# A convolution block and a gated FFN on one core: h of the first and last block in two halves of rows, eleven loads on another queue, another order of first loads

## The chip, the core and the metric

The kernel runs on one core of a Trainium2 chip. The metric is device time in microseconds of one execution, the median over several. The core has a matrix engine (PE; PEld is its weight load), a vector engine (DVE), a scalar engine (ACT), GpSimd (POOL) and SyncE (SP). SP and POOL issue DMAs here, each engine runs its own instructions in the order in which they were built, and an instruction that waits holds up all that stand behind it on its engine.

## What is computed

```python
def _A_ref(q, k, v, shift_k, ssm_k, ssm_D):
    k_shift = sum(k_pad[:, t:t + S, :] * shift_k[:, ks - 1 - t] for t in range(ks))   # 4 taps
    kv = k_shift * v
    y = irfft(rfft(kv, 2S) * rfft(ssm_k, 2S))[:S]     # long causal convolution over the sequence
    y = y + kv * ssm_D
    return q * y

x = A_q                                                 # 2048 x 640
h = x + _A_ref(_layernorm(x), A_k, A_v, A_shift_k, A_ssm_k, A_ssm_D)
h2 = h + (silu(LN(h) @ w_gate) * (LN(h) @ w_up)) @ w_down    # 640 -> 1728 -> 640
```

All arrays are bfloat16. x, k, v are 2048 x 640, ssm_k is 640 x 2048. (B_x is not used.)

## The kernel before

The sequence is cut into four blocks of 512 tokens. A block is held as 128 partitions with 4 rows of 640 each; `ROWS = (1, 3, 0, 2)` is the order in which rows are handled. The convolution is done block by block in a transformed domain. For block j: the kernel piece g (of ssm_k) is turned (`g_turned`, line 396) and transformed (`spectrum`, line 436: G0 to G2; `window_of` for the last); k is loaded transposed into `kT`, the four taps and the product with v are formed (`kv_of`, line 480) and transformed (X0 to X3); `mac` (line 520) multiplies and adds the spectra of all pairs of blocks on DVE, and some of its additions are accumulating DMAs from POOL (`added`, line 234, issued at line 235); `inverse` (line 600) transforms back on PE (i0 to i3, L645), ACT scales each row (z, L652), DVE forms h = (x - mean) * z (L654) with its sum, ACT sums the squares (L568), `ln2` (line 590) makes the layernorm's scale with three small DVE operations and one power on POOL (L572); `turn_h` (line 661) normalizes each row (DVE L668 or ACT L666) and turns it into `hT`, by PE and an eviction for blocks 0 and 3, by DMA transposes for blocks 1 and 2 (`HTURN`). `ln1` (line 574) gets the layernorm of x on ACT and POOL.

`ffn(j)` then multiplies hT by gate and up weights (`proj`, L702: 5 matmuls of 512 columns, one for each 128 of the 640 channels) into PSUM pairs, two chunks of 128 features at once; ACT takes Silu (L714); the product with up goes either through an ACT copy (L717) and DVE (L719) or straight from PSUM on DVE (L718); the down projection (L749) takes 28 matmuls of 320 columns for each row. For blocks 0 to 2 h is stored first and the FFN's output is added to it in DRAM by accumulating DMAs from POOL (L756); the last block's rows are added on DVE (L766, L768) and stored from SP.

A name in `SUM` with 'four' (here i1 to i3, G0 to G2, X1 to X3) uses a form with half as many matmuls and more DVE additions (lines 613 to 634); a name in `DIRECT` (i0, X0) uses matmuls alone.

All operations are declared to a planner (`Plan`) that only replays them: `ORDER` is a list of operation numbers, written out, and each engine gets its instructions in that order. A negative number takes the operation's second form (an eviction on DVE instead of ACT, an addition by DMA instead of on DVE). Loads and stores (`load`, line 237) have one form here and are all issued by SP. Large tiles live in an arena of `UNITS` slots; PSUM has 4 slots of two banks.

Of the kernel before, what the change touches and what calls it, by code (L numbers as in the profile page):

```python
# [16 lines left out]
D = 640  # L17
# [18 lines left out]
DIRECT = ('i0','X0')  # L36
SUM = {'G0':'four','X1':'four','G1':'four','G2':'four','X2':'four','X3':'four','i1':'four','i2':'four','i3':'four'}
# [4 lines left out]
UNITS = 20  # L42
SLOTS = {"row": 4, "z": 2, "sg": 3, "ps": 4, "sm": 10}
ORDER = (
# [40 lines left out]
WHOLE = ((0, 1),)  # L85
ROWS = (1, 3, 0, 2)

# [96 lines left out]
def kernel(ctx: ExitStack, tc: tile.TileContext, A_q, A_k, A_v, A_shift_k, A_ssm_k, A_ssm_D, B_x,  # L184
# [52 lines left out]
    def load(nbytes, fn, w, r=()):  # L237
        return plan.add("sp", nbytes / 370.0, fn, r, w)
# [36 lines left out]
    def load_g(j):  # L275
        b = new("ld")
        load(MB, lambda: nc.sync.dma_start(
            out=ap(b).rearrange("p (c t) -> p c t", c=KT),
            in_=A_ssm_k[0:D, j * BLK:(j + 1) * BLK].rearrange("(c p) t -> p c t", p=P)), [b])
        return b  # L280

    def load_t(src, j):
        b = new("ld")
        load(MB, lambda: nc.sync.dma_start(out=rd(b), in_=block(src, j)), [b])
        return b

    def load_x(j):
        b = new("x")
        load(MB, lambda: nc.sync.dma_start(out=ap(b), in_=block(xq, j)), [b])
        return b  # L290
# [178 lines left out]
    def load_k(j):  # L469
# [5 lines left out]
        for lo in (0, 2):  # L475
            load(MB // 2, lambda lo=lo: nc.sync.dma_start(out=rd(k)[:, lo:lo + 2], in_=block(kk, j)[:, lo:lo + 2, :]), [(k, lo // 2)])
# [418 lines left out]
```

## Time and profile before

| what | value |
|---|---|
| median of 3 runs | 267.63 us (265.11 to 268.7) |
| the profiled execution | 265.97 us |
| its span, first to last instruction | 264.3 us |
| mean granted PE clock | 0.987 |
| busy: DVE, ACT | 204.4 us, 172.5 us |
| DMA | 34.22 MB, mean 130 GB/s |

A line of the profile names source line, engine, operation, tiles and count; the numbers behind are total busy time in us and mean duration in ns, then the idle time ahead of those instructions and what ended it. "Critical" pieces (the chain of waits) give start, length and what ran. PE busy times overlap, since matmuls are pipelined; the pace is read from runs of back-to-back matmuls.

### The profile page before, as it was taken

How to read it: one execution, taken by the hardware profiler on the slowest of the kernel's cores; microseconds unless marked ns; L12 is line 12 of the kernel's file. 1: busy time of each engine (PE TensorE's matmuls, PEld its weight loads, DVE VectorE, ACT ScalarE, POOL GpSimd, SP SyncE). 2: the span in 40 equal slices, each digit the busy share in tenths (PEclk: the TensorE clock that was granted, in tenths of full speed). 3: DMA queues.
4: the chain of work that ended last, by engine and by line, in shares of the span. 5: the costliest groups of instructions: out<-in, count | busy, mean ns of one | idle time of the engine just before them, and what ended most of it. 6: DMA issues, size and time to landing. Idle time of an engine off the chain costs nothing.

```text
span 264.3 us, 4769 instructions
## 1 busy us (share of the span) xinstructions
PE 240.2 (91%) x1914; PEld 138.8 (53%) x1929; DVE 204.4 (77%) x271; ACT 172.5 (65%) x294; POOL 48.8 (18%) x52
## 2 busy tenths in 40 slices
PE   2588989699999999999957999999999999999993
PEld 2455655444455676444423777544456764444771
DVE  3579969899999999998998999999999430222113
ACT  1798999897797994247777974775595834533100
POOL 2000130102122131330061021213228203000000
PEclk9999999799999999999997999999999999999999
DMA  6946899995584527789237906697491225000002
GB/s 220 355 133 104 227 350 218 289 249 99 102 278 146 99 102 148 134 186 145 37 99 127 227 0 139 152 195 127 89 149 14 38 25 72 5 0 0 0 29 74
DMA packets 37731, 34.22 MB, mean 130 GB/s; under 512 B 22406, under 2 KB 32716, under 8 KB 37708
## 3 DMA queue, kind: packets, MB, share of 16 engines
q1 hardware_dynamic: 32716, 24.08, 34.2%
q0 software_dynamic: 4992, 9.83, 23.2%
q8 instruction: 15, 0.25, 0.4%
q14 instruction: 8, 0.07, 0.1%
HBM read 16.21 MB, written 4.59 MB: 79 GB/s over the span
## 4 chain that ended last, share of the span: by engine, by line
PE 41%; DVE 32%; DMA 11%; ACT 7%; issue 6%; SPq 2%; DVEq 0%; ACTq 0%
PE ps L702 21%; DVE arena L524 17%; PE ps L749 13%; PE ps L317 4%; DMA arena<-in_A_v_dram 3%; DMA arena<-arena 3%; DMA arena<-in_A_q_dram 3%; DVE arena L654 2%; ACT arena L400 2%; DMA arena<-in_A_ssm_k_dram 2%; DVE arena L367 2%; PE ps L645 2%; DVE arena L371 2%; PE ps L392 1%; DVE tT L719 1%
## 5 line engine op out<-in xcount | busy, mean ns | idle before, releaser
L702 PE MATMUL ps<-arena,wgu 128*128 128x512 bf16 x506 | 114.6, 379 | 1.2 <-DMA arena<-row 0.4
L524 DVE TENSOR_TENSOR arena<-arena 128x2560 bf16<-128x2560 bf16 (+1 forms) x68 | 91.4, 1369 | 1.5 <-DMA arena<-arena 0.8
L702 PEld LDWEIGHTS <-wgu 128*128 128x128 bf16 x520 | 50.6, 98 | 59.8 <-issue 0.9
L749 PE MATMUL ps<-wd,tT 128*128 128x320 bf16 x448 | 64.0, 299 | 0.9 <-DVE row L768 0.9
L749 PEld LDWEIGHTS <-tT 128*128 128x128 bf16 x448 | 43.6, 98 | 18.5 <-issue 1.1
L714 ACT ACTIVATE sg<-ps 128x1024 bf16<-128x1024 f32 (+1 forms) x28 | 26.8, 961 | 30.0 <-PE ps L702 24.9
L317 PE MATMUL ps<-arena,WF 128*128 128x320 bf16 x160 | 28.8, 302 | 6.8 <-DMA arena<-arena 2.7
L717 ACT CAST sg<-ps 128x1024 bf16<-128x1024 f32 (+1 forms) x23 | 21.9, 952 | 12.4 <-DVE tT L719 5.6
L719 DVE TENSOR_TENSOR tT<-sg,sg 128x1024 bf16<-128x1024 bf16 (+1 forms) x23 | 15.0, 652 | 17.1 <-ACT sg L717 17.1
L235 POOL DMA_DIRECT2D arena<-arena x12 | 14.8, 1307 | 68.3 <-DVE arena L524 27.8
L317 PEld LDWEIGHTS <-WF 128*128 128x128 bf16 x160 | 15.4, 99 | 17.1 <-issue 7.6
L568 ACT ACTIVATE junk<-arena 128x640 bf16<-128x640 bf16 x32 | 23.7, 742 | 0.9 <-DVE arena L654 0.4
L307 ACT CAST arena<-ps 128x320 bf16<-128x320 f32 (+1 forms) x44 | 22.8, 578 | 0.4 <-PE ps L317 0.4
L307 ACT ACTIVATE arena<-ps 128x640 bf16<-128x640 f32 (+1 forms) x29 | 18.6, 667 | 2.3 <-PE ps L317 1.9
L645 PE MATMUL ps<-arena,WI 128*128 128x320 bf16 x96 | 17.1, 320 | 2.8 <-DVE arena L623 2.7
L572 POOL TENSOR_TENSOR sm<-sm,neghalf 128x4 f32<-128x4 f32 x8 | 11.3, 1415 | 37.4 <-DVE sm L595 37.0
L652 ACT ACTIVATE z<-ps,sm 128x640 f32<-128x640 f32 x16 | 12.6, 805 | 4.7 <-POOL sm L572 2.0
L654 DVE SCALAR_TENSOR_TENSOR arena<-arena,sm,z 128x640 bf16<-128x640 bf16 x16 | 13.7, 880 | 1.6 <-ACT z L652 1.5
L583 POOL TENSOR_TENSOR sm<-sm 128x4 f32<-128x4 f32 x4 | 3.9, 966 | 56.9 <-ACT junk L578 56.9
L645 PEld LDWEIGHTS <-WI 128*128 128x128 bf16 x96 | 9.5, 102 | 8.8 <-DVE arena L623 4.0
L756 POOL DMA_DIRECT2D out_dram<-row x12 | 12.2, 1251 | 8.1 <-ACT row L754 8.1
L578 ACT ACTIVATE junk<-arena 128x640 bf16<-128x640 bf16 x16 | 11.9, 742 | 1.7 <-DMA arena<-in_A_q_dram 1.6
(77 smaller groups left out, 204.8 us busy)
## 6 DMA issues: line engine op xcount, KB each, us to landing
arena<-arena POOLq DMA_DIRECT2D x12, 640.0 KB, 6.2
arena<-in_A_q_dram SPq DMA_DIRECT2D x4, 640.0 KB, 5.7
arena<-in_A_v_dram SPq DMA_DIRECT2D x4, 640.0 KB, 7.9
arena<-in_A_ssm_k_dram SPq DMA_DIRECT2D x4, 640.0 KB, 7.0
wd<-in_B_w_down_dram SPq DMA_DIRECT2D x1, 2080.0 KB, 9.5
out_dram<-arena SPq DMA_DIRECT2D x3, 640.0 KB, 5.2
out_dram<-row POOLq DMA_DIRECT2D x12, 160.0 KB, 4.5
wgu<-in_B_w_up_dram SPq DMA_DIRECT2D x1, 800.0 KB
```

What stands on the lines that cost most here:

```text
L235: plan.add("dve", ns, fn, reads, [write], ("add", 2 * P * R * D, lambda: nc.gpsimd.dma_start(out=to(), in_=what(), accum_op=ALU.add, max_d ...
L307: (lambda: nc.scalar.activation(dst(), src(), ACT.Copy, scale=2.0)) if twice else (lambda: nc.scalar.copy(dst(), src())),
L317: nc.tensor.matmul(ap(ps)[:, h, 0:NH], w, ap(src)[:, r, h * NH:(h + 1) * NH], start=(first and i == 0), stop=(last and i == len(rs) - 1), ...
L524: return lambda: f(*(x() for x in args))
L568: act(725, lambda r=r: nc.scalar.activation(ap(junk), ap(x)[:, r, :], ACT.Square, scale=D ** -0.5, accum_out=sm(s, MSQ, (r,))), [(x, r)], ...
L645: nc.tensor.matmul(ap(ps)[:, w, 0:NH], m, src[:, w * NH:(w + 1) * NH], start=(i == 0), stop=(i == len(terms) - 1))
L654: dve(740, lambda r=r, z=z: v.scalar_tensor_tensor(ap(x)[:, r, :], ap(x)[:, r, :], sm(n1, MEAN, (r,)), ap(z), op0=ALU.subtract, op1=ALU.mu ...
L702: nc.tensor.matmul(ap(ps)[:, i, :], w(k), ap(hT)[:, k, :], start=(k == 0), stop=(k == KT - 1))
L714: act(905 if two_ else 490, lambda: nc.scalar.activation(of(sg), of(*gate), ACT.Silu), [(gate[0], gate[1] + i) for i in range(m)], [sg])
L717: op = plan.add("act", 905 if two_ else 490, lambda: nc.scalar.copy(of(co), of(*up)), psu + [sg], [co] + tt, ("dve", 1135 if two_ else 600 ...
L719: op.rest = dve(602 if two_ else 336, lambda: nc.vector.tensor_mul(to(), of(sg), of(co)), [sg, co], tt)
L749: nc.tensor.matmul(ap(ps)[:, hf, 0:NH], ap(tT)[:, c, at:at + P], ap(wd)[:, c, hf * NH:(hf + 1) * NH], start=(c == 0), stop=(c == NCH - 1))
```

## The change

1. For blocks 0 and 3 (`LEAD = {0: 4, 3: 2}`) `inverse` makes the statistics of h in two halves of two rows each, with a `sm` tile, three DVE operations and one power of their own, and `turn_h` uses them so. The first 4 (block 0) or 2 (block 3) groups of the gate and up projections are done on 256 tokens at a time: matmuls of 256 columns, two groups of features sharing a PSUM tile.
2. Every load has a second form issued by GpSimd (`"pq"`). ORDER takes it for eleven: x of blocks 1 to 3, v of block 1, g of block 2, one weight piece of 800 KB, both loads of `w_down`, the h store of block 1, and two output stores of the last block.
3. ORDER is a new list throughout. The first loads on SP are x, ssm_D, taps, g, WF (the transform's basis), k in two pieces, g of block 1, v, WI; before they were k, taps, k, x, v, g, g of block 1, ssm_D, WF, WI. The warm-up matmuls stand first on PE; before they stood between i0 and the FFN. In the new list five PSUM copies more are on ACT and fewer on DVE, and 13 additions instead of 12 are DMAs.
4. i1 is no longer 'four': 32 instead of 16 matmuls, without six DVE additions. The arena has 21 slots instead of 20.

In the whole program there are 120 matmuls of 512 columns less and 240 of 256 more, and 16 of 320 more.

```diff
-DIRECT = ('i0','X0')
-SUM = {'G0':'four','X1':'four','G1':'four','G2':'four','X2':'four','X3':'four','i1':'four','i2':'four','i3':'four'}
+DIRECT = ('X0', 'i0')
+SUM = {'G0': 'four', 'X1': 'four', 'G1': 'four', 'G2': 'four', 'X2': 'four', 'X3': 'four', 'i2': 'four', 'i3': 'four'}
...
-UNITS = 20
+LEAD = {0: 4, 3: 2}
+UNITS = 21
...
+HALVES = (ROWS[:2], ROWS[2:])
...
     def load(nbytes, fn, w, r=()):
-        return plan.add("sp", nbytes / 370.0, fn, r, w)
+        return plan.add("sp", nbytes, lambda: fn(nc.sync), r, w, ("pq", nbytes, lambda: fn(nc.gpsimd)))
...
-        s = new("sm")
-        for r, ps in out.items():
-            z = new("z")
...
-        square_sums(x, s, ROWS)
-        ln2(s, ROWS)
-        return s
+        stats = []
+        for rs in HALVES if LEAD.get(j) else (ROWS,):
+            s = new("sm")
+            for r in rs:
+                ps, z = out[r], new("z")
...
+            square_sums(x, s, rs)
+            ln2(s, rs)
+            stats += [(r, s) for r in rs]
+        return stats
...
+        lead = LEAD.get(j, 0)
...
+        def proj(ps, i, w, src, rs=ROWS):
+            lo, n = ROWS.index(rs[0]) * P, len(rs) * P
+
             def mm():
                 for k in range(KT):
-                    nc.tensor.matmul(ap(ps)[:, i, :], w(k), ap(hT)[:, k, :], start=(k == 0), stop=(k == KT - 1))
-            pe(1079, mm, src + [hT], [(ps, i)])
+                    nc.tensor.matmul(split(ap(ps), n)[:, i, :], w(k), ap(hT)[:, k, lo:lo + n], start=(k == 0), stop=(k == KT - 1))
+            pe(1079 if n == BLK else 546, mm, src + [(hT, r) for r in rs], [(ps, i)])
...
+        def chunks(gis, rs):
             g, u = new("ps"), new("ps")
...
+            for b, gi in enumerate(gis):
+                for a, ps in enumerate((g, u)):
+                    for i in range(2):
+                        f0 = (2 * gi + i) * P
+                        proj(ps, 2 * b + i, lambda k, a=a, f0=f0: ap(wgu)[:, k, a, f0:f0 + P], [(wgu, (group(f0), a))], rs)
+            gate_up(2 * gis[0], 2 * len(gis), (g, 0), (u, 0), rs)
...
+        for gi in range(0, lead, 2):
+            chunks((gi, gi + 1), HALVES[0])
+        if j == 0:
+            for gi in range(0, lead, 2):
+                chunks((gi, gi + 1), HALVES[1])
+        for gi in range(lead, NGRP - 1):
+            chunks((gi,), ROWS)
+        odd_chunks()
+        if j:
+            for gi in range(0, lead, 2):
+                chunks((gi, gi + 1), HALVES[1])
```

ORDER's new list is left out here, and so are the many calls of `load` that only hand on the queue.

More of the change, by code (lines that the diff above doesn't have):

```diff
@@ L283, in load_t @@
         b = new("ld")
-        load(MB, lambda: nc.sync.dma_start(out=rd(b), in_=block(src, j)), [b])
+        load(MB, lambda q: q.dma_start(out=rd(b), in_=block(src, j)), [b])
         return b
@@ L288, in load_x @@
         b = new("x")
-        load(MB, lambda: nc.sync.dma_start(out=ap(b), in_=block(xq, j)), [b])
+        load(MB, lambda q: q.dma_start(out=ap(b), in_=block(xq, j)), [b])
         return b
@@ L475, in load_k @@
         for lo in (0, 2):
-            load(MB // 2, lambda lo=lo: nc.sync.dma_start(out=rd(k)[:, lo:lo + 2], in_=block(kk, j)[:, lo:lo + 2, :]), [(k, lo // 2)])
+            load(MB // 2, lambda q, lo=lo: q.dma_start(out=rd(k)[:, lo:lo + 2], in_=block(kk, j)[:, lo:lo + 2, :]), [(k, lo // 2)])
         for r in range(R):
@@ L662, in turn_h @@
+        return stats
+    def turn_h(x, stats, j):
         hT = new("hT")
-        for r in ROWS:
+        for r, s in stats:
             hn = new("row")
             at = ROWS.index(r)
-            plan.add("act", 815, lambda r=r, hn=hn: nc.scalar.activation(ap(hn), ap(x)[:, r, :], ACT.Identity, bias=sm(s, OFF, (r,)), scale=sm(s, RSTD, (r,))),
+            plan.add("act", 815, lambda r=r, hn=hn, s=s: nc.scalar.activation(ap(hn), ap(x)[:, r, :], ACT.Identity, bias=sm(s, OFF, (r,)), scale=sm(s, RSTD, (r,))),
@@ L693, in ffn, with split @@
         if not end:
-            load(MB, lambda: nc.sync.dma_start(out=block(oo, j), in_=ap(h)), [there], [h])
+            load(MB, lambda q: q.dma_start(out=block(oo, j), in_=ap(h)), [there], [h])
         def done(cs, rs):
             return (tT, frozenset((c, r) for c in cs for r in rs))
-        def proj(ps, i, w, src):
+        lead = LEAD.get(j, 0)
+        def split(t, n):
+            return t.rearrange("p a (b n) -> p (a b) n", n=n)
+        def proj(ps, i, w, src, rs=ROWS):
+            lo, n = ROWS.index(rs[0]) * P, len(rs) * P
@@ L706, in gate_up @@
             sg, co = new("sg"), new("sg")
+            lo, n = ROWS.index(rs[0]) * P, len(rs) * P
             def of(b, at=0):
-                return ap(b)[:, at:at + m, :]
+                return split(ap(b), n)[:, at:at + m, :]
             def to():
-                return ap(tT)[:, c:c + m, :]
-            two_ = m == 2
-            act(905 if two_ else 490, lambda: nc.scalar.activation(of(sg), of(*gate), ACT.Silu), [(gate[0], gate[1] + i) for i in range(m)], [sg])
+                return ap(tT)[:, c:c + m, lo:lo + n]
@@ L715, in gate_up @@
+            wide_ = m * n > BLK
+            act(905 if wide_ else 490, lambda: nc.scalar.activation(of(sg), of(*gate), ACT.Silu), [(gate[0], gate[1] + i) for i in range(m)], [sg])
             psu = [(up[0], up[1] + i) for i in range(m)]
-            tt = [done(range(c, c + m), ROWS)]
-            op = plan.add("act", 905 if two_ else 490, lambda: nc.scalar.copy(of(co), of(*up)), psu + [sg], [co] + tt,
-                          ("dve", 1135 if two_ else 600, lambda: nc.vector.tensor_mul(to(), of(sg), of(*up))))
@@ L730, in ffn @@
-        for a in range(2):
-            proj(ps, a, lambda k, a=a: ap(wgu)[:, k, a, f0:f0 + P], [(wgu, (group(f0), a))])
-        gate_up(NC_FULL - 1, 1, (ps, 0), (ps, 1))
-        last_ps, sg, up = new("ps"), new("sg"), new("sg")
-        proj(last_ps, 0, lambda k: ap(wodd)[:, k], [wodd])
-        act(490, lambda: nc.scalar.activation(ap(sg)[0:64, 0, :], ap(last_ps)[0:64, 0, :], ACT.Silu), [(last_ps, 0)], [sg])
-        act(490, lambda: nc.scalar.copy(ap(up)[0:64, 0, :], ap(last_ps)[64:P, 0, :]), [(last_ps, 0)], [up])
@@ L737, in ffn @@
-        dve(336, lambda: nc.vector.tensor_mul(ap(tT)[0:64, NC_FULL, :], ap(sg)[0:64, 0, :], ap(up)[0:64, 0, :]), [sg, up], [done([NC_FULL], ROWS)])
+            tt = [done(range(c, c + m), rs)]
+            op = plan.add("act", 905 if wide_ else 490, lambda: nc.scalar.copy(of(co), of(*up)), psu + [sg], [co] + tt,
+                          ("dve", 1135 if wide_ else 600, lambda: nc.vector.tensor_mul(to(), of(sg), of(*up))))
+            op.rest = dve(602 if wide_ else 336, lambda: nc.vector.tensor_mul(to(), of(sg), of(co)), [sg, co], tt)
@@ new lines, in chunks, with odd_chunks @@
+        def chunks(gis, rs):
+            g, u = new("ps"), new("ps")
+            for b, gi in enumerate(gis):
[4 more added lines that the diff above has]
+            gate_up(2 * gis[0], 2 * len(gis), (g, 0), (u, 0), rs)
+        def odd_chunks():
+            ps = new("ps")
+            f0 = (NC_FULL - 1) * P
+            for a in range(2):
+                proj(ps, a, lambda k, a=a: ap(wgu)[:, k, a, f0:f0 + P], [(wgu, (group(f0), a))])
+            gate_up(NC_FULL - 1, 1, (ps, 0), (ps, 1))
+            po, sg, up = new("ps"), new("sg"), new("sg")
+            proj(po, 0, lambda k: ap(wodd)[:, k], [wodd])
+            act(490, lambda: nc.scalar.activation(ap(sg)[0:64, 0, :], ap(po)[0:64, 0, :], ACT.Silu), [(po, 0)], [sg])
+            act(490, lambda: nc.scalar.copy(ap(up)[0:64, 0, :], ap(po)[64:P, 0, :]), [(po, 0)], [up])
+            dve(336, lambda: nc.vector.tensor_mul(ap(tT)[0:64, NC_FULL, :], ap(sg)[0:64, 0, :], ap(up)[0:64, 0, :]), [sg, up], [done([NC_FULL], ROWS)])
@@ L769, in ffn @@
                 dve(740 if len(hs) == 2 else 407, out_of, [(ps, hf) for hf in hs] + [(h, r), (n1, cells(MEAN, (r,)))], [(o, hf) for hf in hs])
[L770 removed]
+                load(MB // 4 // (3 - len(hs)), lambda q, r=r, o=o, lo=lo, n=n: q.dma_start(out=block(oo, j)[:, r, lo:lo + n], in_=ap(o)[:, lo:lo + n]),
                      [], [(o, hf) for hf in hs])
@@ L794 @@
     dve(350, fold, [ident], [eye])
-    load(P * KT * 8, lambda: nc.sync.dma_start(out=ap(taprow), in_=A_shift_k.rearrange("(c p) t -> c (p t)", p=P)), [taprow])
+    load(P * KT * 8, lambda q: q.dma_start(out=ap(taprow), in_=A_shift_k.rearrange("(c p) t -> c (p t)", p=P)), [taprow])
     pt = new("ps")
@@ L812 @@
     x = load_x(0)
-    load(P * R * 4 * P * 2, lambda: nc.sync.dma_start(out=ap(WI), in_=wi_h.ap()), [WI])
+    load(P * R * 4 * P * 2, lambda q: q.dma_start(out=ap(WI), in_=wi_h.ap()), [WI])
     minus = new("minus")
```

37 lines of the change are left out of this document (13 added, 24 removed), and 82 rows, old and new, of the table ORDER.

## The prediction, made before the changed kernel was run

> **What bounds the kernel now.** I read the page's totals first, then the windows of 10 us, then the chain of waits, and last the timeline of the first 54 us.
>
> ```profile
> span 264.3 us, 4769 instructions
> ...
> PE 240.2 (91%) x1914; PEld 138.8 (53%) x1929; DVE 204.4 (77%) x271; ACT 172.5 (65%) x294; POOL 48.8 (18%) x52
> ```
>
> ```profile
> 10.00:20.00 10.00, 6.63 (x66) 4.18 (x67) 7.96 (x19) 9.84 (x22) 0.00 (x0) 1.00 0.65 215
> ...
> 30.00:40.00 10.00, 8.96 (x174) 6.32 (x167) 7.62 (x11) 9.83 (x17) 3.41 (x4) 1.00 1.16 331
> ...
> 130.00:140.00 10.00, 7.26 (x34) 3.15 (x32) 9.90 (x12) 8.44 (x12) 5.44 (x5) 0.92 0.21 66
> 140.00:150.00 10.00, 8.16 (x156) 5.35 (x155) 9.03 (x16) 8.58 (x15) 0.00 (x0) 0.91 0.96 182
> ...
> 190.00:200.00 10.00, 9.95 (x57) 5.47 (x57) 9.86 (x9) 9.10 (x17) 4.88 (x5) 1.00 0.63 100
> ...
> 220.00:230.00 10.00, 9.95 (x47) 4.58 (x47) 1.11 (x2) 4.67 (x6) 2.29 (x3) 1.00 0.40 51
> ```
>
> The columns are busy times of PE, PEld, DVE, ACT and POOL, then PE's clock, the DMA share and GB/s. There are three stages with three limits. Up to 50 us ACT is full (9.84 and 9.83 of 10). From there to 200 us DVE is full and PE nearly so. After 200 us DVE is almost empty and PE alone is full. The chain of waits gives PE's true pace, since each of its pieces is a back-to-back run:
>
> ```profile
> 64.42 10.76 PE ps L702 x49
> ...
> 77.77 1.11 PE ps L489 x112
> ...
> 131.51 4.75 DMA arena<-in_A_ssm_k_dram
> 136.33 2.52 ACT arena L400
> ...
> 200.78 0.72 PE ps L645 x4
> ...
> 205.58 6.52 PE ps L749 x48
> 212.10 0.56 PE ps L392 x10
> ...
> 260.83 0.55 DVE row L768
> ```
>
> So a matmul of 512 columns takes 10.76/49 = 0.2196 us, one of 320 takes 6.52/48 = 0.1358, a transpose 0.056, a tap 0.0099. The row at 200.78 is the first matmul of i3, the inverse transform of the last block; DVE work ends just ahead of it, and PE runs from there to the end. I therefore cut the span at two points: S, the first FFN matmul, and I, the first matmul of i3.
>
> ```profile
> 2.11 0.52 POOL L781 MEMSET tT<- 64x512 bf16 x1
> ...
> 8.83 0.74 ACT L578 ACTIVATE junk<-arena 128x640 bf16<-128x640 bf16 x1 [1.57 <-DMA arena<-in_A_q_dram]
> ...
> 28.72 0.52 SPq L284 DMA_DIRECT2D arena<-in_A_v_dram  x1
> ...
> 30.04 0.50 SPq L289 DMA_DIRECT2D arena<-in_A_q_dram  x1
> ...
> 31.91 0.81 POOL L583 TENSOR_TENSOR sm<-sm 128x4 f32<-128x4 f32 x1 [29.29 <-ACT junk L578]
> ...
> 40.04 0.88 DVE L654 SCALAR_TENSOR_TENSOR arena<-arena,sm,z 128x640 bf16<-128x640 bf16 x1
> ...
> 44.98 0.88 DVE L654 SCALAR_TENSOR_TENSOR arena<-arena,sm,z 128x640 bf16<-128x640 bf16 x1
> ...
> 53.52 3.40 PE L702 MATMUL ps<-arena,wgu 128*128 128x512 bf16 x14
> ```
>
> S is 53.5. Between S and I lie 147.3 us. In the built order that stretch holds 405 matmuls of 512, 358 of 320 (254 of the down projection, 72 forward, 32 inverse) and 280 taps: 88.9 + 48.6 + 2.8 = 140.3 us. PE loses 7.0 us there. After I lie 63.5 us with 135 of 512, 210 of 320 and 20 transposes: 29.6 + 28.5 + 1.1 = 59.3 us, and 4.2 of tail.
>
> **The last block (LEAD 3: 2).** In the changed order, after I stand 95 matmuls of 512, 80 of 256, 182 of 320 and 20 transposes. A matmul of 256 is not in the trace. Its floor is half of 512, 0.110. Its ceiling is that plus a weight load that is not hidden:
>
> ```profile
> L702 PEld LDWEIGHTS <-wgu 128*128 128x128 bf16 x520 | 50.6, 98 | 59.8 <-issue 0.9
> ...
> L626 DVE TENSOR_TENSOR arena<-arena 128x640 bf16<-128x640 bf16 x12 | 5.4, 487 | 0.1
> L623 DVE TENSOR_TENSOR arena<-arena 128x1280 bf16<-128x1280 bf16 x6 | 4.7, 822 | 0.1
> ...
> L719 DVE TENSOR_TENSOR tT<-sg,sg 128x1024 bf16<-128x1024 bf16 (+1 forms) x23 | 15.0, 652 | 17.1 <-ACT sg L717 17.1
> ...
> L718 DVE TENSOR_TENSOR tT<-sg,ps 128x1024 bf16<-128x1024 bf16 (+1 forms) x5 | 5.6, 1111 | 6.3 <-PE ps L702 6.3
> ...
> L394 DVE COPY arena<-ps 128x640 bf16<-128x640 bf16 x8 | 3.7, 483 | 2.0 <-PE ps L392 2.0
> ```
>
> 0.098 more on 240 of them would be 23.5 us, but the transposes at 212.10 have a load each and pass in 0.056, so I take 0.110, and the halving costs nothing. The stretch after I is then 20.9 + 8.8 + 24.7 + 1.1 = 55.5 us, 3.8 less than now: 28 down-projection matmuls of block 2 have moved ahead of I. That is possible because the first two rows' statistics no longer wait for the other two. Between i3's first matmul and the first transpose of h stand 8.5 us of PE work instead of 11.3 (200.78 to 212.10). The chain that this work must cover:
>
> ```profile
> L568 ACT ACTIVATE junk<-arena 128x640 bf16<-128x640 bf16 x32 | 23.7, 742 | 0.9 <-DVE arena L654 0.4
> ...
> L652 ACT ACTIVATE z<-ps,sm 128x640 f32<-128x640 f32 x16 | 12.6, 805 | 4.7 <-POOL sm L572 2.0 <-PE ps L645 1.4 <-DVE arena L654 1.2
> ...
> L572 POOL TENSOR_TENSOR sm<-sm,neghalf 128x4 f32<-128x4 f32 x8 | 11.3, 1415 | 37.4 <-DVE sm L595 37.0
> ```
>
> 0.7 of matmuls, then on ACT three z of 0.81 and two squares of 0.94 (0.742 and the read of the sum), a power of 1.4 and about 0.8 of small DVE steps with the row itself: 7.2 us. No hole opens; were the cover 1 us short, the end would move by that. Each split block also adds one power on POOL and three DVE operations on two columns, beside full PE.
>
> **Work between S and I.** It gains those 28 (3.8 us); 16 more matmuls in i1, which loses its 'four' form (2.2); and 8 forward matmuls and 10 transposes that used to stand ahead of S (1.1 + 0.6). So it is 140.3 + 7.7 = 148.0 us of PE. On DVE i1 saves 4 x 0.487 + 2 x 0.822 = 3.6 us and five PSUM copies that go to ACT 2.4. One addition (1.49) goes to a DMA. Small statistics (six more, 1.0), four more products straight from PSUM at 1.1 for four fewer behind an ACT copy at 0.65 (1.9) and one doubled copy (0.8) give back about 3.7: DVE is 3.8 us lighter. ACT gains five copies and loses four in the gate groups: nil.
>
> **The start (S).** Three things move it. x goes first, past two k halves of 640 KB in all: at 342 GB/s (below) 2.0 us off the 8.83 at which ACT starts. ACT's queue ahead of the last z of block 0, which frees the PSUM that FFN needs, is 2.7 us shorter than ahead of S now (g of block 2 is copied later, 2.5; one square less, 0.9; one more eviction, 0.7). ACT is full there, so this counts: S = 53.5 - 2.0 - 2.7 = 48.8. The halves agree: the second L654 ends at 40.9, the fourth at 45.9 (0.88 after their starts), and 45.9 to 53.5 is 7.6, so 40.9 + 7.6 = 48.5.
>
> Against it stands the move to GpSimd's queue. In the changed order v and x of block 1, g of block 2 and one weight piece stand right behind the making of ident on POOL, with no semaphore to wait for. POOL has nothing to do from 2.6 to 31.9 us, so it will issue them at once, where SP now sends v and x at 28.7 and 30.0. That is 3 x 640 + 800 KB = 2.79 MB beside the first loads:
>
> ```profile
> 6.00:8.00 2.00, 1.83 (x19) 1.44 (x17) 0.93 (x3) 0.69 (x1) 0.00 (x0) 1.00 0.95 342
> ...
> 10.00:12.00 2.00, 0.00 (x0) 0.00 (x0) 1.45 (x3) 1.94 (x5) 0.00 (x0) 1.00 1.08 384
> 12.00:14.00 2.00, 1.68 (x38) 1.37 (x39) 1.90 (x5) 1.91 (x6) 0.00 (x0) 1.00 1.03 388
> ```
>
> The DMA share is already 0.95 to 1.08 there. At 342 GB/s the four take 8.2 us. If they only filled gaps they would cost 0; if all went ahead of g, basis, k and v, 8.2. x is out before them and ACT has its sums to do meanwhile, so I take half, 4.1, and S = 52.9. The Trainium skill (DMA: Bandwidth & Descriptors, Rules for kernel authors) speaks against this part: it says that spreading DMAs over the issuing engines gives no bandwidth, since all run on the same 16 engines, and saves only issue time. Taken alone it would put the cost nearer the upper end; no run here shows two queues loading at the start.
>
> **The tail.** Two of the last stores go to POOL behind two late accumulates. Their issue is bounded by these rows:
>
> ```profile
> L235 POOL DMA_DIRECT2D arena<-arena x12 | 14.8, 1307 | 68.3 <-DVE arena L524 27.8 <-issue 11.7 <-DVE arena L371 10.2
> ...
> L756 POOL DMA_DIRECT2D out_dram<-row x12 | 12.2, 1251 | 8.1 <-ACT row L754 8.1
> ```
>
> ```profile
> out_dram<-row POOLq DMA_DIRECT2D x12, 160.0 KB, 4.5
> ```
>
> ```profile
> 249.96 7.35 PE ps L749 x54
> ```
>
> The third tile's output is ready about 3.3 us before the last full row's matmuls end; four issues of 1.25 and 4.5 us to landing (counted from the issue) end 4.9 us after that point. The tail now runs 7.0 us from there (257.3 to 264.3), so 2 us of margin hide it: nothing. The other POOL loads add 1.3 us of issue each to an engine that is 18% busy. Behind the h store of block 1 waits one power, whose squares take ACT 0.9 meanwhile: nothing, at worst 1.3.
>
> **Sum.** PE allows I at 52.9 + 148.0 = 200.9. DVE allows 200.8 - 3.8 - 0.6 = 196.4, so for the first time PE is the later one. I add 1.5 us for what remains of the 7.0 that PE loses now (between 0 and 7.0; the largest piece, the late g of block 3 at 131.51 with ACT's copy behind it, depends on order). I = 202.4, and the end is 202.4 + 63.5 - 3.8 = 262.1, against 264.3. The profiled execution took 265.97, so 1.7 lies around the span: 263.8. That execution is 0.6% under the median of 267.63; I put the number for a median between, 264.5, about 1% faster.
>
> **Rivals.**
> Faster: the four loads fit into gaps. S = 48.8, PE allows 196.8, I = 198.3, the end 258.0, the run 259.7, 2.4% faster. For it: x is out first, and ACT has 4 us of sums of x. Against it: the DMA share of 1.0 up to 14 us.
> Slower: the four loads go ahead. g, basis, k and v come 8.2 us later, S = 57.0; ACT, DVE and PE then reach the same waits out of step and PE loses its 7.0 us again: I = 212.0, the end 271.7, the run 273.4, 2.8% slower. It decides from a delay of about 6 us in v. For it: v is last in SP's row and all of X0 hangs on it. A page of the Trainium skill (DMA: Bandwidth & Descriptors, Queues, rings and completion order) says that each engine takes turns between queues by packets, so that a queue with large rows (x and v, 5 KB) would outrun g with its 1 KB rows; that is this rival.
> No gain: the start comes out as forecast, but PE loses 7.0 us as now, for the freed DVE time was not what held it. I = 207.9, the end 267.6, the run 269.3, 1.2% slower.
>
> **Chances.** Forecast 0.42 (its own range 261 to 267.5), loads in gaps 0.27, loads ahead 0.18, no gain 0.13. Two per cent, 5.3 us, is about what a measurement of this kernel can tell from no change. Faster by more: the second case and the low end of the first, 0.33. Slower by more: the third and a little of the fourth, 0.22. Within: 0.45. The range reaches from the second case with less than 1.5 us of stalls, 257.5, to near the third, 272.5.
>
> **What would show it.** POOL issues four loads before 9 us; g's first transpose comes after 9 us, v's product after 20; first FFN matmul at 53 (49 or 57 in the rivals); a 256-column matmul paced at 0.110; first i3 matmul near 202 with PE, not DVE, ahead of it in the chain; from there 59.7 us to the end. A pace near 0.2 for 256 columns, or a hole in PE between i3 and the transposes of h, would make the prediction wrong.

## The result, and the profile after

The changed kernel takes 286.1 us (median of 4 runs, 283.5 to 287.1) against 268.1 for the kernel before on the same chip: a ratio of 1.078, 95% interval 1.072 to 1.084. The forecast was 264.5 with a range up to 272.5. In a later series of 4 runs it took 281.8 against 266.3, 1.059 (1.045 to 1.074). It is 6 to 8% slower, and the forecast was wrong.

The totals of its profiled execution (285.0 us):

```profile
span 283.3 us, 5062 instructions
...
PE 249.6 (88%) x2052; PEld 153.8 (54%) x2065; DVE 201.2 (71%) x266; ACT 172.8 (61%) x294; POOL 56.8 (20%) x66
```

DVE is 3.2 us lighter (3.8 forecast); PE's busy time is 9.4 us longer, partly because matmuls at a low clock last longer. The windows (same columns as before: PE, PEld, DVE, ACT, POOL, PE's clock, DMA share, GB/s) show where:

```profile
10.00:20.00 10.00, 4.91 (x35) 3.37 (x36) 2.52 (x6) 3.03 (x6) 0.00 (x0) 0.50 1.04 379
20.00:30.00 10.00, 8.68 (x172) 5.46 (x170) 7.82 (x20) 8.56 (x18) 0.35 (x1) 0.50 0.40 120
70.00:80.00 10.00, 8.53 (x62) 4.07 (x63) 6.84 (x7) 5.67 (x13) 1.31 (x1) 0.83 0.59 83
170.00:180.00 10.00, 5.35 (x39) 3.62 (x38) 8.99 (x7) 2.38 (x3) 2.85 (x4) 0.87 0.87 177
180.00:190.00 10.00, 8.85 (x35) 3.86 (x35) 3.94 (x5) 5.12 (x9) 1.05 (x2) 0.79 0.55 92
```

In the second 10 us DVE works 2.52 instead of 7.96 and ACT 3.03 instead of 9.84, beside a DMA share of 1.04. Two more bad stretches follow, at 70 to 80 and at 170 to 190 us, each with a lower clock. PE's timeline names what ended its waits (in brackets):

```profile
56.51 7.80 PE L716 MATMUL ps<-arena,wgu 128*128 128x256 bf16 x70 [0.46 <-DVE arena L398]
...
71.41 4.01 PE L716 MATMUL ps<-arena,wgu 128*128 128x512 bf16 x10 [2.30 <-ACT sg L729]
96.56 1.26 PE L649 MATMUL ps<-arena,WI 128*128 128x320 bf16 x8 [1.40 <-DVE arena L615]
...
120.87 2.32 PE L716 MATMUL ps<-arena,wgu 128*128 128x512 bf16 x9 [1.65 <-DMA arena<-row]
...
179.79 0.58 PE L716 MATMUL ps<-arena,wodd 128*128 128x512 bf16 x1 [4.65 <-DMA arena<-row]
```

The first row is S, 56.5 instead of the forecast 52.9. It also gives the pace of 256 columns: 7.80/70 = 0.111 us. The fourth and fifth are the first FFN matmuls of blocks 1 and 2, which wait for h's DMA transposes. Call these two points F1 and F2. They cut the stretch from S to I once more, and that turns out to matter. The ten matmuls of 512 in 4.01 us at 71.4 show what a hole costs beyond itself: at full pace they take 2.2.

| stretch | PE work before | took | PE work after | took, first profile | took, second profile |
|---|---|---|---|---|---|
| start to S | | 53.5 | | 56.5 | 52.9 |
| S to F1 | 51.7 | 52.4 | 55.5 | 64.4 | 64.4 |
| F1 to F2 | 53.0 | 59.5 | 53.0 | 58.9 | 58.6 |
| F2 to I | 35.6 | 35.4 | 39.4 | 42.1 | 42.1 |
| I to end | 59.3 | 63.5 | 55.5 | 61.4 | 61.4 |
| span | | 264.3 | | 283.3 | 279.4 |

PE work is the count of matmuls between two cuts in the built order times the paces of the prediction (0.111 for 256 columns). S, F1, F2 and I are starts read from the timeline. The 19.0 us of the first profile are +3.0, +12.0, -0.6, +6.7 and -2.1. Only the start differs between the two profiles; everything behind S repeats to 0.3 us. All tables of stretches here are read from one profiled execution each, which can lie some us above its kernel's median, so they are read beside the ratios of the medians.

### The profile page after: what moved, and what is told of

The parts are those of the page before. It is cut to its first block, busy times and chain, and to the rows that moved or that the text cites. A ratio compares the mean times of both kernels' runs of the same rounds, so it can differ in the third digit from the quotient of the medians.

```text
span 283.3 us, 5062 instructions
## 1 busy us (share of the span) xinstructions
PE 249.6 (88%) x2052; PEld 153.8 (54%) x2065; DVE 201.2 (71%) x266; ACT 172.8 (61%) x294; POOL 56.8 (20%) x66
## 4 chain that ended last, share of the span: by engine, by line
PE 52%; DMA 19%; issue 9%; ACT 7%; DVE 7%; SPq 3%; POOL 2%; DVEq 0%; ACTq 0%; POOLq 0%
PE ps L716 30%; PE ps L778 10%; DMA arena<-arena 6%; DMA WF<-const_wf 5%; PE ps L649 5%; DMA arena<-row 5%; PE ps L321 4%; DMA out_dram<-row 3%; SPq L389 3%; PE ps L493 2%; DVE arena L528 2%; POOL sm L576 1%; PE ps L396 1%; ACT sg L732 1%; ACT junk L572 1%
## 5 line engine op out<-in xcount | busy, mean ns | idle before, releaser
L716 PE MATMUL ps<-arena,wgu 128*128 128x512 bf16 (+1 forms) x630 | 118.9, 344 | 7.8 <-ACT sg L729 5.1
L716 PEld LDWEIGHTS <-wgu 128*128 128x128 bf16 x640 | 63.0, 99 | 59.5 <-issue 13.0
L528 DVE TENSOR_TENSOR arena<-arena 128x2560 bf16<-128x2560 bf16 (+1 forms) x66 | 88.1, 1364 | 1.2 <-PE ps L321 0.5
L321 PE MATMUL ps<-arena,WF 128*128 128x320 bf16 x160 | 32.1, 324 | 3.0 <-DMA arena<-arena 1.1
L732 ACT CAST sg<-ps 128x1024 bf16<-128x1024 f32 (+1 forms) x19 | 18.5, 971 | 10.7 <-PE ps L716 10.2
L572 ACT ACTIVATE junk<-arena 128x640 bf16<-128x640 bf16 x32 | 23.7, 742 | 0.8 <-DVE arena L660 0.4
L733 DVE TENSOR_TENSOR tT<-sg,ps 128x1024 bf16<-128x1024 bf16 (+1 forms) x9 | 9.8, 1100 | 18.9 <-PE ps L716 18.0
L576 POOL TENSOR_TENSOR sm<-sm,neghalf 128x4 f32<-128x4 f32 (+1 forms) x10 | 12.9, 1292 | 49.2 <-DVE sm L599 48.9
L311 ACT ACTIVATE arena<-ps 128x640 bf16<-128x640 f32 (+1 forms) x27 | 17.6, 669 | 3.3 <-PE ps L321 3.0
L734 DVE TENSOR_TENSOR tT<-sg,sg 128x1024 bf16<-128x1024 bf16 (+1 forms) x19 | 12.5, 658 | 8.1 <-ACT sg L732 8.0
L783 ACT ACTIVATE row<-ps,sm 128x640 bf16<-128x640 f32 x12 | 9.4, 789 | 12.3 <-PE ps L778 8.8
```

The source lines that it names most:

```text
L311: (lambda: nc.scalar.activation(dst(), src(), ACT.Copy, scale=2.0)) if twice else (lambda: nc.scalar.copy(dst(), src())),
L321: nc.tensor.matmul(ap(ps)[:, h, 0:NH], w, ap(src)[:, r, h * NH:(h + 1) * NH], start=(first and i == 0), stop=(last and i == len(rs) - 1), ...
L528: return lambda: f(*(x() for x in args))
L572: act(725, lambda r=r: nc.scalar.activation(ap(junk), ap(x)[:, r, :], ACT.Square, scale=D ** -0.5, accum_out=sm(s, MSQ, (r,))), [(x, r)], ...
L576: nc.gpsimd.tensor_tensor(sm(s, RSTD, rs), sm(s, VAR, rs), ap(neghalf)[:, 0:len(rs)], op=ALU.pow)
L716: nc.tensor.matmul(split(ap(ps), n)[:, i, :], w(k), ap(hT)[:, k, lo:lo + n], start=(k == 0), stop=(k == KT - 1))
```

## Experiments

Each median stands with its ratio to the kernel before, run beside it, and the 95% interval of that ratio. Four runs do one operation several times over; none leaves any out. The theories are named in the expectations as they came up. Line numbers shift by a few lines where a kernel has lines more.

**The start and the queue.** Four runs of the changed order, and a control with the order of before. gate holds the four early loads back:

```diff
+            if i == -200:
+                self.gate(self.ops[25].bufs[0])
             if op.fn:
...
+    plan.gate = lambda b: nc.gpsimd.tensor_copy(ap(late), rd(b)[:, 3, 0:1])
```

> The changed kernel, with one copy of a single column of v of block 0 on GpSimd ahead of its four early loads, so that they start only when v has landed (before: at 2.4 to 4.5 us). Nothing else moves. Theory A (the four loads that run ahead are the cause: they take the DMA engines from g, the basis, k and v, DVE falls 10 us behind by 30 us, and since DVE still limits the stretch up to i3, most of that reaches the end): v's product moves from 25.7 to about 16 us, the first FFN matmul from 56.5 to 49 to 51, the first i3 matmul from 222 to 205 to 210, the run 268 to 275. Theory B (the order itself is out of step: row slots held by accumulating DMAs and h's DMA transposes on SP cost the 17 us between the first FFN matmul and i3): the start gains 6 us but the hole at 170 to 190 us stays, run 280 to 283. Theory C (the clock at 0.5 from 10 to 30 us is the cost, whatever the loads): the clock stays low and the run stays over 283.

all_sp only changes entries of ORDER back to their first form (the second form of operation 199 is written -200), so that all eleven go out from SP:

```diff
-    -200, -201,
+    199, 200,
...
-    -404,
+    403,
...
-    -904, 894, 604, -894,
+    903, 894, 604, 893,
```

> The changed kernel with all eleven loads and stores back on SP's queue, in the order in which the kernel lists them. The two loads of block 1 then stand right behind the first loads and the inverse basis on SP, g of block 2 and the weight piece behind DMA transposes. Theory A: the first loads come in their own order again, S at 49 to 52, run 266 to 274, that is as the gated kernel less 3 us for the tail. Theory B: about 280, as the middle of the order is unchanged. A run more than 5 us under the gated kernel would say that the later loads on GpSimd (down projection, x of blocks 2 and 3, the store of h) cost time too; more than 5 us over it, that SP's queue cannot carry them.

tail_sp does that for the last line alone (operations 903 and 893), and after_again is the changed kernel unaltered.

> The changed kernel with the two last stores of full rows back on SP's queue. Theory: the store from GpSimd, issued behind two accumulates, holds the row slot into which the last row's halves are written (0.56 issue and 3.4 us of DMA stand in the chain at 273.5 to 277.5), so the end comes 3 us earlier, run about 283. Rival: the last row's matmuls end at 280 whatever the store does, and nothing changes, 286.

> The changed kernel itself, a second time. In the run with the two stores back on SP the start was 4.7 us earlier (first FFN matmul at 51.9) than in the first profile of the changed kernel (56.5), though nothing differs there. If the start varies between executions, this run lies between 279 and 287 and its first FFN matmul anywhere from 51 to 57, and the two stores are worth nothing by themselves (the stretch from i3 to the end was 61.7 us with them on SP, 61.2 on GpSimd). If the start is fixed, it is 286 again, and the tail's stores did 6 us in some other way.

Measured: gate 278.8 us, 1.043 (1.035 to 1.051); all_sp 272.4, 1.021 (1.014 to 1.029); tail_sp 279.9, 1.045 (1.036 to 1.055); after_again 281.8, 1.059. The stretches:

| kernel | S | S to F1 | F1 to F2 | F2 to I | I to end | span |
|---|---|---|---|---|---|---|
| gate | 51.7 | 64.0 | 58.2 | 42.1 | 61.3 | 277.4 |
| tail_sp | 51.9 | 65.3 | 59.0 | 42.1 | 61.7 | 280.0 |
| all_sp | 48.3 | 63.3 | 55.5 | 42.7 | 61.7 | 271.5 |

The issues by queue (KB each, us from issue to landing) show what changes for the first loads. Of the changed kernel:

```profile
arena<-in_A_k_dram SPq DMA_DIRECT2D x2, 320.0 KB, 16.2
...
WF<-const_wf SPq DMA_DIRECT2D x1, 512.0 KB, 15.3
```

Of all_sp:

```profile
arena<-in_A_k_dram SPq DMA_DIRECT2D x2, 320.0 KB, 8.4
...
WF<-const_wf SPq DMA_DIRECT2D x1, 512.0 KB, 7.9
```

In all_sp v and x of block 1 are issued nearly as early (7.2 and 9.0 us), but behind the first loads on the same queue, while g of block 2 and the weight piece go out only from 30.5 us on; k and the basis land in half the time. Which of the two, the one queue or the fewer bytes, does how much of this was not separated. The issue of v of block 0 from SP, too, lasts 5.86 us in the changed kernel (4.78 to 10.64) and 1.48 in all_sp (from 5.11). In the changed kernel POOL's row of issues is as forecast:

```profile
2.37 0.72 POOL L288 DMA_DIRECT2D arena<-in_A_v_dram  x1
3.09 0.56 POOL L293 DMA_DIRECT2D arena<-in_A_q_dram  x1
3.63 0.90 POOL L281 DMA_DIRECT2D arena<-in_A_ssm_k_dram  x1
4.52 0.89 POOL L688 DMA_DIRECT2D wgu<-in_B_w_up_dram  x1
```

DVE's first product with v starts at 25.7 us in the changed kernel's first profile (22.6 in the second), 17.8 in all_sp. Gate brings it to 17.2, yet S stays at 51.7: the four loads, let go at 15.9 us, make the next 10 us bad instead (DMA share 1.16, DVE busy 6.32 from 20 to 30 us). Theory A is right for the start: S was 51.6 to 56.5 in five profiles with this start (mean 53.0) and 45.9 to 48.3 in six with all on SP (mean 47.1), a price of some 6 us. It is wrong for the rest, since the 64 us from S to F1 do not shrink and gate ends between the two forecasts. all_sp lands in theory A's range and 6.4 us under gate, so by its expectation the later loads on GpSimd cost time as well. The hole at 170 us stays in gate, as theory B had it, though B's row slots turn out not to be its reason. Theory C, the clock by itself, falls with 278.8.

tail_sp shows a trap in reading. In the changed kernel's chain of waits the store from POOL stands right on the path:

```profile
272.29 0.89 DVE row L795
...
273.48 0.56 POOL out_dram L799
...
274.04 3.40 DMA out_dram<-row
...
277.46 0.56 DVE row L797
...
278.07 2.08 PE ps L778 x14
```

Without it, in tail_sp, the place of those 4 us is taken by PE:

```profile
263.90 9.12 PE ps L778 x67
...
273.84 0.55 DVE row L797
...
274.43 2.08 PE ps L778 x14
```

From I to the end it takes 61.7 us, not 61.4: the store was a second path of the same length, and moving it gains nothing. That tail_sp and after_again differ by 2 us lies within their intervals.

**The control.** The order of before, with the same four loads from POOL at the start (ahead), and held back (ahead_held).

```diff
-UNITS = 20
+UNITS = 21
...
-        load(MB, lambda: nc.sync.dma_start(out=rd(b), in_=block(src, j)), [b])
+        load(MB, lambda: (nc.gpsimd if j == 1 else nc.sync).dma_start(out=rd(b), in_=block(src, j)), [b])
```

> The kernel before, with 21 units instead of 20 and the same four loads (v and x of block 1, g of block 2, one 800 KB weight piece) sent from GpSimd's queue at the start, without a wait; the order on PE, ACT and DVE is that of before. Theory A: g, basis, v land late, DVE falls behind by 5 to 10 us in the first 30 us, and the run goes to 273 to 279. Theory B: the order of before absorbs it, at most 3 us, 267 to 271.

> The kernel before with 21 units and the four loads sent from GpSimd, but held back by a copy of one column of v of block 0, so that they start when v has landed. It has the same slots as the run in which the four went at once (285.8 us, in which x of block 2 was sent at 128.7 instead of 113.9 us, a second difference). Theory A: most of that run's 19 us go away, 266 to 272. Rival: what cost there was the changed slots (x of block 2 and h of block 2 late), and the run stays over 278.

285.8 us, 1.067 (1.057 to 1.077), and 285.0, 1.072 (1.063 to 1.081). In the first run both theories missed; in the second the rival, over 278, came true. S comes at 58.3 and 57.5 and F1 at 115.1 in both. From F1 to F2 it then takes 72.6 and 68.1 us, since to place the four loads early their arena slots had to be taken early, and x of block 2 got a slot that is free only at 128.7 us (113.9 before). The kernel was meant to change one thing and changed two; it shows that the order of before is hurt too, but not by how much for the loads alone.

**Row slots.** taprow and drow are put into tiles that are written later, and the space goes to two more slots.

```diff
-SLOTS = {"row": 4, "z": 2, "sg": 3, "ps": 4, "sm": 10}
+SLOTS = {"row": 6, "z": 2, "sg": 3, "ps": 4, "sm": 10}
...
+    taprow = Buf(None, None, ap(tT)[0:KT, 0, :])
+    drow = Buf(None, None, ap(wodd)[0:1].rearrange("p k a q -> p (k a q)"))
```

> The changed kernel with six row slots in place of four (the taps' and D's rows of the start lie in tT and wodd, which are not written until later). Theory B1: in the changed order block 0's output rows and h of block 1, and block 1's first output row and h of block 2, want the same four slots at the same time; ACT then waits in order for a DMA transpose or an accumulate to let go of a slot, and h's DMA transposes, which FFN 1 and FFN 2 wait for, go out late. With six slots PE's waits for h (6.3 us in two holes, plus some 3 us of low clock behind them) shrink to 0 to 2, the stretch from the first FFN matmul to the first i3 matmul goes from 165.5 to 156 to 159, the run to 276 to 280. Rival B2: h itself is late, since DVE and ACT are behind; the slots are free but the holes stay, 284 to 287.

> All eleven loads and stores on SP's queue (272.4 us) and six row slots. Theory B1: the stretch between the two cuts goes from 161.5 to 153 to 156, the run to 264 to 267, level with the kernel before. Rival B2: 271 to 273.

rows6: 281.4 us, 1.061 (1.048 to 1.073) against 1.059 for after_again, no gain; S to F1 took 65.6 and F1 to F2 60.9. The wait for a slot went, and another stood behind it. The chain of rows6:

```profile
91.79 13.88 DMA arena<-in_A_q_dram
...
105.76 0.84 ACT junk L582 x2
106.62 0.83 ACT junk L582 x2
107.45 2.44 ACT row L673 x3
...
113.86 3.21 DMA arena<-row
...
117.21 3.16 PE ps L716 x10
```

x of block 2, sent by POOL, takes 13.9 us to land, and ACT's sums of its rows stand ahead of the rows of h in ACT's order. With all on SP the six slots gave 269.5, 1.011 (1.007 to 1.016) against 1.021 (1.014 to 1.029), with overlapping intervals; its stretches are 62.7, 55.9, 42.7 and 61.6. That lies between the forecasts of B1 and B2. Theory B1 falls: the slots are not what the 12 us from S to F1 consist of. This kernel (S 47.5, span 270.5) is the base of the runs that follow.

**Three guesses at what is left.** The copy of block 2's g on POOL instead of ACT; v of block 0 ahead of g of block 1; both. And, on the gated kernel, the down projection's weights on SP.

```diff
-            act(2414, lambda: nc.scalar.copy(ap(by_r).rearrange("q a b -> q (a b)").rearrange("q (r c p) -> q r c p", r=R, c=KT),
+            act(2414, lambda: (nc.gpsimd.tensor_copy if j == 2 else nc.scalar.copy)(ap(by_r).rearrange("q a b -> q (a b)").rearrange("q (r c p) -> q r c p", r=R, c=KT),
```

> All eleven loads and stores on SP and six row slots (269.5 us, 1.011), and the copy of block 2's g made by GpSimd, which is idle then, instead of ACT. Theory D: what is left of the loss stands on ACT's queue at the first FFN groups: squares, this copy of 2.5 us and the table load of 1.3 us stand ahead of the first Silu, PE has no free PSUM and stops (4.6 us of waits for Silu up to 64 us, and 2 us of low clock behind), DVE falls back 5 us between 60 and 90 us, and h of block 2 comes as much later. Without the copy PE's wait for Silu there falls from 5.0 to 2 or 3, the stretch between the two cuts from 161.4 to 156 to 159, the run to 264 to 267. Rival: ACT's other work in that place (evictions of kv of block 2, squares) holds PE all the same: 268 to 271.

> All on SP and six row slots, and v of block 0 sent ahead of g of block 1, which nothing needs before 20 us. Theory: the order of the first loads still costs; DVE stands 2.8 us behind the kernel before at 20 us (8.1 of 20 us busy, against 10.9). v lands 1.9 us earlier (640 KB at 342 GB/s), the first FFN matmul goes from 47.5 to 46 to 47, and DVE passes that on: run 267 to 268.5. Rival: ACT, not v, holds the start: no change, 269 to 270.

> All on SP, six row slots, the copy of g of block 2 on GpSimd, and v of block 0 ahead of g of block 1. If theory D and the order of the first loads both hold, 262 to 265, faster than the kernel before (266.3); if neither, 268 to 270.

> The changed kernel with the four early loads held back until v has landed (278.8 us) and, beside that, the two loads of the down projection's weights back on SP. Theory E: on GpSimd's queue x of block 2 stands behind 2.1 MB of those weights (13.9 us from issue to landing, and ACT's squares of block 2 wait for it in order, ahead of h of block 1), so that part of the gap to the kernel with everything on SP (272.4) is this one load: 275 to 277, and the stretch between the cuts 161 to 163. Rival: the queue does not matter there, 278 to 280.

271.6 us, 1.018 (1.012 to 1.024); 272.0, 1.018 (1.011 to 1.024); 272.2, 1.017 (1.012 to 1.023); and 279.2, 1.037 (1.028 to 1.046) against 1.043 for gate. None gains. g2pool shows why. Its timeline, ahead of and behind the place where PE waited:

```profile
55.45 0.45 PE L396 MATMUL ps<-ident,row 128*128 128x128 bf16 x5 [2.08 <-DVE row L675]
...
62.23 2.32 PE L716 MATMUL ps<-arena,wgu 128*128 128x512 bf16 x10 [2.56 <-ACT sg L729]
```

ACT is 6.0 us busy from 50 to 60 us instead of 9.9, S is 45.6, 2 us earlier than in the base (S varies by 2.4 us between the kernels with all on SP and the same start), and PE, done earlier with the first half, now waits 2.1 us for the rows of the second half, which DVE makes between products of block 1. The wait for Silu, which theory D gave to the copy, stays at 2.6 us. F1 is at 109.2 instead of 110.2, and the ratio is no better than the base's. Theory D, and the order of the first loads, explain nothing that can be measured; theory E's load of weights neither.

**Which engine sets which stretch.** One operation is done several times over, so that one engine has about 3 us more to do. Theory F is that DVE sets the stretch, theory G that it does not.

```diff
+AGAIN = {263: 3}
...
             if op.fn:
-                op.fn()
+                for _ in range(AGAIN.get(op.n, 1)):
+                    op.fn()
```

(263: 3 is dve1; 375: 4 pe1; 191: 5 act1; 488: 3 dvem.)

> All on SP, six row slots (269.5 us, 1.011), and one product of block 1 on DVE done three times over (2.9 us more on DVE, between the first FFN matmul and i1; the result is the same). F: i1 and h of block 1 come 2.5 to 3 us later, and the end 2 to 3 us: 271.5 to 273. G: DVE has 4 us idle there, the end moves by less than 1.

> The same kernel with one gate chunk of FFN 0 done four times over (15 matmuls of 512 more, 3.3 us on PE, at about 60 us). F: PE's holes ahead of i1 and of h of block 1 take them up; the first FFN 1 matmul and the end move by less than 1 us: 269 to 270.5. G: the end moves by 3: 272 to 273.5.

> The same kernel with one weight copy on ACT done five times over (2.9 us more on ACT, at about 73 us). F: ACT is not what i1 waits for: less than 1 us, 269 to 270.5. G for ACT: 2 to 3 us: 271.5 to 273.

> The same kernel with one product of block 2 on DVE done three times over (2.9 us more on DVE, between h of block 1 and i2). F: h of block 2 and FFN 2's first matmul come 2.5 to 3 us later and so does the end: 271.5 to 273. G: PE is full between 112 and 163 us, DVE's lag is hidden: less than 1.

| kernel | S | S to F1 | F1 to F2 | F2 to I | S to I | ratio |
|---|---|---|---|---|---|---|
| base | 47.5 | 62.7 | 55.9 | 42.7 | 161.3 | 1.011 (1.007 to 1.016) |
| DVE, S to F1 | 48.0 | 62.9 | 55.7 | 42.7 | 161.4 | 1.012 (1.001 to 1.023) |
| PE, S to F1 | 46.4 | 65.0 | 56.0 | 41.8 | 162.8 | 1.021 (1.013 to 1.029) |
| ACT, S to F1 | 45.9 | 64.5 | 55.5 | 42.7 | 162.7 | 1.026 (1.017 to 1.036) |
| DVE, F1 to F2 | 46.8 | 62.9 | 58.4 | 41.0 | 162.4 | 1.025 (1.015 to 1.036) |

From S to F1 extra DVE work vanishes; PE's and ACT's come through, by 2.3 and 1.8 of some 3 us. In act1 the work on ACT becomes a new hole on PE:

```profile
76.24 0.71 PE L718 MATMUL ps<-arena,wgu 128*128 128x256 bf16 x5 [2.61 <-ACT arena L313]
```

From F1 to F2 extra DVE work comes through (2.5 of 2.9), and then 1.7 are won back behind F2. So neither F nor G alone: G, with PE and ACT in turn, holds up to F1, F from there to F2. For each engine one operation in one place was tried, so another place may answer otherwise; the interval of the last row just touches that of the base.

**The halves, and the last load.** whole_first keeps the 256-token groups but makes and turns both halves of h first (in ORDER, 179, 183, 184, 180 and 181 are moved up behind 182). x3_sp is the changed kernel with one load back on SP.

```diff
-    -617,
+    616,
```

> All on SP, six row slots (269.5 us), with the second half of h of block 0 made and turned ahead of FFN 0's first group; the groups of 256 tokens stay. The first FFN matmul then comes at 55 to 57 instead of 47.5. Theory H: the early first half is 7.8 us of PE work that only moves a hole, since ACT, which makes both halves, is full from 40 to 62 us: the first FFN 1 matmul stays within 3 us of 110.2 and the run within 3 us of 269.5. Rival: the early start is worth what it moves, first FFN 1 matmul at 117 to 119, run 276 to 279.

> The changed kernel with one load, x of block 3, back on SP's queue, where it stands behind the four DMA transposes of h of block 2. Theory E2: from GpSimd it goes out beside them and takes their share of the DMA engines (6.9 us from the last transpose's issue to its landing; 3.3 with all on SP), so the stretch from FFN 1's to FFN 2's first matmul falls from 58.9 to 55.5 to 56.5 and the run by 2 to 3 us (279 to 282 against 281.8 to 286). Rival: the transposes are late for another reason, 58 to 59 as before.

whole_first: 279.0 us, 1.056 (1.047 to 1.065). S is at 54.6, F1 at 115.9, 5.7 us later than the base. Its timeline:

```profile
53.60 1.25 PE L396 MATMUL ps<-ident,row 128*128 128x128 bf16 x10 [8.05 <-DVE row L675]
69.51 2.32 PE L716 MATMUL ps<-arena,wgu 128*128 128x512 bf16 x10 [2.40 <-ACT sg L729]
```

The early half is worth most of what it moves, against theory H (F1 comes just under the rival's 117). The 2.4 us wait for Silu stays with whole h, so the halves are not its cause either.

x3_sp: 277.5 us, 1.048 (1.042 to 1.055), F1 to F2 56.4, S 52.4. In the chain of the changed kernel, the last DMA transpose of h of block 2:

```profile
172.72 6.93 DMA arena<-row
```

and in x3_sp:

```profile
169.48 3.39 DMA arena<-row
```

POOL sent x of block 3 at 171.99 us, beside the transposes; SP sends it behind them, at 170.8, with the last transpose already issued from 169.5 on. Theory E2 holds for the stretch: this one load cost about 2.5 us there. The run's median is a little under the 279 to 282 of the forecast, and its interval meets that of after_again.

## Why the prediction was wrong

- **Pace of 256 columns**: 0.111, as taken (0.110).
- **The four loads at the start**: issued at 2.4 to 4.5 us, as said. The forecast took 4.1 us, half of 8.2, and S = 52.9. Five profiles with this start give 51.6 to 56.5. With all on SP, S is 45.9 to 48.3, where the forecast without these loads was 48.8. The term is some 6 us, so the mechanism was right and the size a little low. That S = 52.9 nearly met the mean of 53.0 is in part luck: S without the loads came 1.7 us earlier than forecast. By the Trainium skill (DMA: Bandwidth & Descriptors, Rules for kernel authors) issuing from more engines gives no bandwidth, which put the cost nearer the upper end. The trace agrees: 379 GB/s from 10 to 20 us with two queues, where one queue gave 384 and 388 in two windows of 2 us before, while k and the basis landed 7 to 8 us later than in all_sp.
- **x first**: ACT started at 4.8, 4 us earlier, better than the 2.0 taken, and then stood idle from about 9 to 15 us.
- **PE work from S to I**: 148.0 by count, and that is right (55.5 + 53.0 + 39.4 = 147.9).
- **The step that failed** is the sum "PE allows I at 52.9 + 148.0 = 200.9" with "1.5 us for what remains of the 7.0 that PE loses now". PE lost 17.5 us there in the first profile. The sum let the old holes shrink and allowed for no new ones. In the kernel before, 6.5 of the 7.0 us were lost between F1 and F2, in two holes at i2 and in the low clock around them (0.92 and 0.91 from 130 to 150 us):

```profile
137.93 2.31 PE L645 MATMUL ps<-arena,WI 128*128 128x320 bf16 x9 [2.74 <-DVE arena L623]
...
143.88 4.53 PE L317 MATMUL ps<-arena,WF 128*128 128x320 bf16 x32 [1.84 <-DMA arena<-arena]
```

These holes did go, as the forecast hoped: in the changed kernel PE is 9.74 to 10.00 us busy in each 10 us from 130 to 170. But a new hole of 4.65 us stands ahead of F2, where PE waits for the DMA transposes of h of block 2, so that F1 to F2 loses 5.9 us again. From S to F1 PE had lost 0.7 and now loses 8.9, with 3.8 us more to do: 6.0 are waits (2.3 for Silu, 1.7 at i1, 1.65 at F1 and one of 0.36), most of the rest is the low clock behind them. From F2 to I it had lost nothing; now it loses 2.7, with 3.8 more to do (the 28 matmuls taken from behind I): 1.1 are waits, the rest is the low clock behind the hole at F2 (0.79 from 180 to 190 us). That PE, not DVE, stands ahead of I in the chain came true.
- **"The freed DVE time"**: DVE's bound for I (196.4) took DVE as the limit all the way. dve1 shows, on the base, that up to F1 it isn't: there 2.9 us more on DVE lengthen the stretch by 0.2, so freeing DVE should buy little there; that was not run.
- **POOL's later loads**: priced as 1.3 us of issue on an idle engine, "nothing, at worst 1.3". The issue was harmless, the place in the queue was not: with the loads on SP F1 to F2 takes 55.5 instead of 58.9, 2.5 of it from x of block 3.
- **After I**: 61.4, forecast 59.7. The work fell by 3.8 as counted, the tail grew from 4.2 to 5.9: 1.2 us is a new hole in FFN 3's first groups (PE waits for Silu behind a row copy on ACT until 238.8), and the last row waits 1.5 for DVE instead of 0.9. Between i3 and the transposes of h no hole opened, and the two last stores from POOL cost nothing that tail_sp could show, as said.
- **The rivals**: "slower" had the right sign and part of the mechanism, the loads ahead, but gave it 273.4; most of the loss was not in it. "No gain" had the losses staying at 7.0; 17.5 lies far outside it. No rival had new holes between S and I.

The account with all loads on SP is 7.2 us over the kernel before: -5.3 at the start, +10.9, -4.0, +7.4, -1.8. Of the +10.9 up to F1, 3.8 are counted work; PE's waits there (4.9 in all, 2.2 of them for Silu, the rest mostly at i1 and F1) and the low clock behind them make most of the other 7. Which of ACT's tasks would have to move to close them was not settled: taking one away (g2pool) moved the hole to another wait. One rival stands untried. In the base's chain of waits two of the additions that POOL makes by DMA fill 17.6 of the 21 us from 64.1 to 85.1, ahead of i1:

```profile
64.14 10.42 DMA arena<-arena
...
74.65 2.90 DVE arena L528 x2
...
77.84 7.18 DMA arena<-arena
...
85.12 1.50 DVE arena L615
```

In the changed kernel one of 8.3 us stands there; in the kernel before the chain has none between S and F1. No run put one of them back on DVE. What the 28 moved matmuls cost by themselves was not tried either. No version here beats the kernel before.

## What to carry to other kernels

Sum an engine's work between the points where it must wait for another engine, not over a whole stage. A new order can close one hole and open another of the same size elsewhere, and a sum over the stage shows neither. Moving a load to an idle engine's queue removes the order in which it stood behind other transfers; ask of each what it will run beside. And before calling a store or a copy in the chain of waits a cost, look for a second path of the same length: adding 3 us of work to one engine at a time helps to tell which one sets a stretch.

## Hardware behaviour that was not expected

The start of the changed kernel loses clock as well as time. The clock granted to PE fell to 0.50 from 10 to 30 us in the first profile (0.50 and 1.00 in the second, 1.00 and 1.00 before), though the nine warm-up matmuls ran up to 6.5 us; PE was idle for 8.1 us behind them. A short hole can be followed by the same. In the base kernel PE waits 2.3 us for Silu at 60 us; the windows of 2 us there (PE's busy time first, its clock third from the end):

```profile
60.00:62.00 2.00, 0.12 (x1) 0.00 (x0) 1.80 (x2) 2.00 (x4) 0.00 (x0) 1.00 1.68 175
62.00:64.00 2.00, 1.58 (x4) 0.55 (x4) 2.00 (x3) 0.37 (x1) 0.00 (x0) 0.50 0.51 117
64.00:66.00 2.00, 2.00 (x7) 0.66 (x5) 1.33 (x2) 0.58 (x1) 1.41 (x1) 0.65 1.07 351
```

The clock is half for some 2 us behind it, and the next ten matmuls of 512 take 3.77 us instead of 2.2, so this hole cost 1.7 times its length. The Trainium skill (TensorE: Matmul & The Clock Gate, Part 1: The HAM clock gate) lets the clock drop behind an idle window of about 3.4 us; here it dropped behind 2.3 us, and the measurement decides. Length alone does not settle it: in the kernel before, PE waited 2.35 us up to 12.32 us, and the clock stayed at 1.00. What else it takes was not tried.

The same start, executed five times, put S anywhere from 51.6 to 56.5 us while two queues loaded; on one queue the spread was 45.9 to 48.3.
